# Two weight-gradient stores of a decode backward kernel, cut by rows into pieces

## The chip, the cores and the metric

The kernel runs on one core of a Trainium2 chip. The metric is the device time of one execution in microseconds; three runs of the kernel before took 736.78, 735.42 and 736.70 us, a median of 736.7. A profile of one further execution shows what each engine and each DMA queue did. The engines are TensorE (PE), VectorE (DVE), ScalarE (ACT), GpSimd (POOL) and SyncE (SP). The core has 16 DMA engines, and a DMA is issued from a queue of SyncE, GpSimd or ScalarE.

## The reference

One decode step (one token) through a parallel block, and its whole backward pass. In short:

```python
xn = layernorm(x)                                  # x: [1, 1, 640]
q = (xn @ wq) -> 32 heads of 128                   # wq: [640, 4096]
p = softmax(q . k_cache * 128**-0.5)               # k_cache, v_cache: [32 heads, 8192, 128]
o = p @ v_cache
out = x + o @ wo + (silu(xn @ w1) * (xn @ w3)) @ w2   # wo: [4096, 640], w1, w3: [640, 1728]
grads = vjp(out)(grad_out)   # of x, k_cache, v_cache, wq, wo, w1, w3, w2
```

Everything is bf16 in HBM. The caches are 64 MiB each, and their gradients are as large, so about 268 of the 303.5 MB that move are caches and cache gradients. The gradients of `wq` and `wo` are outer products: `d_wo` is the attention output times `grad_out`, `d_wq` is `xn` times the gradient of `q`.

## The kernel before

The work goes head by head, 32 heads in 8 groups of 4. A head's K and V (2 MB each, one DMA of 128 rows of 16 KB) lie in two of ten SBUF slots. `head(h)` transposes them on TensorE, makes scores, softmax and the sums for the gradients, and runs beside it, on VectorE, the outer products of the head before (`outers_a`, `outers_b`): these write the gradient of V and K over the slot itself. `store` (line 473) sends the slot to HBM from GpSimd's queue, and then asks SyncE's queue to load the next K or V into the same slot. That load waits until the store has landed. A separate block at head 2 does the gated MLP.

The order on each queue is the order of the program text (a manual schedule). GpSimd issues all stores of 128 rows and also the loads of the weights of later groups; SyncE issues the K and V loads. Each queue is served in order.

Per group there is a tile `wq_g` (128 rows, 5 pieces of 512 columns, 5,120 bytes a row) and a tile `wo_g` (128 rows, 4 pieces of 640 columns, also 5,120 bytes a row), each 640 KB, in three buffers that are used in turn. Their life:

- `load_group(g + 2)` (lines 109 to 114, called at line 698 in the last head of group g) loads both from GpSimd's queue. The buffer was group g-1's, so the load of `wq_g` waits until the `wq` gradient of group g-1 has landed, and everything behind it on GpSimd waits with it.
- `fin_wo(g)` (line 501, called from `side_v` in the first head of group g+1) writes the `wo` gradient over `wo_g` with four VectorE instructions and stores it by one DMA (line 505).
- `fin_wq(g, ci)` (line 507) does the same for `wq` in five steps, `ci` 0 to 4, spread over the second and third head of group g+1. The last is called from `side_m`, behind the store of V and ahead of the store of K of the head before, and issues one DMA (line 514).
- Group 7 is finished behind the last head, at lines 819 to 823.

Of the kernel before, what the change touches and what calls it, by code (L numbers as in the profile page):

```python
# [16 lines left out]
P = 128  # L17
# [4 lines left out]
def kernel(  # L22
# [22 lines left out]
    nc = tc.nc  # L45
# [8 lines left out]
    GH = 4  # L54
    NG = H // GH
    GW = GH * DH
# [23 lines left out]
    dwq_v = out_4.rearrange("(ci p) n -> p ci n", p=P)  # L80
    dwo_v = out_5.rearrange("(h p) c -> p h c", p=P)
# [110 lines left out]
    def out_row(vec, mat):  # L192
        k = mat.shape[0]
        for e in range(2):
            nc.tensor.matmul(acc[64 * e:64 * (e + 1), 0:DHALF], lhsT=vec.to_broadcast([k, 64]),
                             rhs=mat[:, e * DHALF:(e + 1) * DHALF], start=False, stop=True, skip_group_check=True)
# [292 lines left out]
    def fin_pe(g):  # L489
# [8 lines left out]
        for hh in range(GH):  # L498
            out_row(G_["od_bf"][:, hh, 0:1], G_["wo"][:, hh, :])

    def fin_wo(g):
        G_ = grp[g]
        for hh in range(GH):
            nc.vector.tensor_scalar(G_["wo"][:, hh, :], g_bc[:], G_["od"][:, hh, 0:1], None, ALU.mult)
        nc.gpsimd.dma_start(dwo_v[:, g * GH:(g + 1) * GH, :], G_["wo"][:])

    def fin_wq(g, ci):
        G_ = grp[g]
        wq_g, dqb = G_["wq"], G_["dqb"]
        nc.vector.scalar_tensor_tensor(wq_g[:, ci, :], wq_g[:, ci, :], 1.0, dqb, ALU.mult, ALU.mult,  # L510
                                       accum_out=dxa[:, ci, g:g + 1])
        nc.vector.tensor_scalar(wq_g[:, ci, :], dqb, xn_col[:, ci:ci + 1], None, ALU.mult)
        if ci == NC - 1:
            nc.gpsimd.dma_start(dwq_v[:, :, g * GW:(g + 1) * GW], wq_g[:])
            grp.pop(g)

    def wrow(wi, ci):
# [147 lines left out]
    def side_k(h):  # L665
        g, hh = divmod(h, GH)
        if hh == 1 and g > 0:
            fin_wq(g - 1, 0)
        elif hh == 2 and g > 0:
            fin_wq(g - 1, 3)  # L670
        elif hh == 3 and g + 1 < NG:
            prep_do(g + 1, 1)

    def side_m(h):
        g, hh = divmod(h, GH)
        if hh == 0 and g > 0:
            fin_od(g - 1)
        elif hh == 1 and g > 0:
            fin_wq(g - 1, 1)
        elif hh == 2 and g > 0:  # L680
            fin_wq(g - 1, 4)
        elif hh == 3 and g + 1 < NG:
            prep_do(g + 1, 2)
            prep_do(g + 1, 3)

    def side_v(h):
        g, hh = divmod(h, GH)
        if hh == 0 and g > 0:
            fin_wo(g - 1)
        elif hh == 1 and g > 0:  # L690
            fin_wq(g - 1, 2)
        elif hh == 2 and g + 1 < NG:
            prep_new(g + 1)
            prep_do(g + 1, 0)
        elif hh == 3 and g + 1 < NG:
            prep_cm(g + 1, hd[h]["m"][:, 324:324 + 4 * GH])
        if hh == 3 and g > 0 and g + 2 < NG:
            load_group(g + 2, nc.gpsimd)
# [120 lines left out]
    fin_od(NG - 1)  # L819
    fin_pe(NG - 1)  # L820
    fin_wo(NG - 1)
    for ci in range(NC):
        fin_wq(NG - 1, ci)
# [58 lines left out]
```

## Time and profile before

| what | us |
|---|---|
| median of three runs | 736.7 |
| the profiled execution | 735.86 |
| its span (first to last instruction) | 734.1 |
| PE busy / DVE busy / ACT busy / POOL busy | 601.6 / 460.3 / 375.5 / 64.7 |
| mean clock granted to TensorE | 0.917 of full |
| GpSimd's store of `wo_g`, issue to landing, median of 8 | 51.0 |
| GpSimd's store of `wq_g`, issue to landing, median of 8 | 48.6 |
| GpSimd's store of a K or V gradient, median of 64 | 45.2 |
| SyncE's load of K / of V, median of 32 each | 18.7 / 22.3 |

The page's second part cuts the span in 40 slices and gives the mean busy share of the 16 DMA engines in each, and the GB/s that they moved:

```profile
DMA  8999999999999999999999999999999999999991
GB/s 351 402 413 419 426 425 419 430 429 430 427 429 421 427 426 427 423 427 425 428 429 413 427 427 423 422 428 428 428 427 413 427 426 429 428 420 430 423 410 79
HBM read 151.34 MB, written 151.34 MB: 412 GB/s over the span
```

A DMA row of 9 in a slice means that the engines were busy 90% of the time or more. TensorE, the busiest compute engine, is busy 82% of the span.

### The profile page before, as it was taken

To read this page: it belongs to the slowest core of one execution; us is meant where nothing else is said; L and a number is where in the kernel's file an instruction comes from. 1 tells how busy PE (TensorE), PEld (TensorE's weight loads), DVE (VectorE), ACT (ScalarE), POOL (GpSimd) and SP (SyncE) were. 2 spreads that over 40 slices of the span, in tenths; PEclk is the share of its full clock that TensorE was granted. 3 is DMA by queue.
4 is the path that set the end of the run, shared out by engine and by line. 5 is a ranking of instruction groups with operands and counts; after the bars stand their busy time and mean duration, and the time that the engine had idled before them with its cause. 6 is when DMAs were issued, how large, how long until landed. Compare 5 with 4: busy or idle time off the path is not lost.

```text
span 734.1 us, 13013 instructions
## 1 busy us (share of the span) xinstructions
PE 601.6 (82%) x5186; PEld 374.7 (51%) x5193; DVE 460.3 (63%) x811; ACT 375.5 (51%) x727; POOL 64.7 (9%) x109
## 2 busy tenths in 40 slices
PE   4988589999899899988897869878798797886920
PEld 2556466665565566544554545544464454554510
DVE  4279637687867776767475555667367674664780
ACT  3641646655666666654454446544465453554500
POOL 0110100001011100200010100201002000001010
PEclk9996799999999999999899989999899998998955
DMA  8999999999999999999999999999999999999991
GB/s 351 402 413 419 426 425 419 430 429 430 427 429 421 427 426 427 423 427 425 428 429 413 427 427 423 422 428 428 428 427 413 427 426 429 428 420 430 423 410 79
DMA packets 27134, 303.52 MB, mean 413 GB/s; under 512 B 2798, under 2 KB 4146, under 8 KB 10434
## 3 DMA queue, kind: packets, MB, share of 16 engines
q0 software_dynamic: 14944, 160.52, 52.0%
q1 hardware_dynamic: 12126, 142.17, 46.0%
q8 instruction: 41, 0.67, 0.3%
q14 instruction: 19, 0.16, 0.1%
q10 hardware_dynamic: 4, 0.00, 0.0%
HBM read 151.34 MB, written 151.34 MB: 412 GB/s over the span
## 4 chain that ended last, share of the span: by engine, by line
DMA 30%; PE 28%; issue 17%; another core or an unknown queue 11%; DVE 7%; ACT 3%; POOL 1%; SPq 0%; POOLq 0%; ACTq 0%; DVEq 0%
DMA wo_g<-in_A_wo_dram 16%; PE pT L314 13%; DMA out_dram<-kv 8%; DMA kv<-in_A_k_cache_dram 4%; PE sA L335 4%; PE X L429 2%; PE dA L335 2%; DMA kv<-in_A_v_cache_dram 2%; DVE kv L462 2%; PE m L352 1%; ACT kv L624 1%; DVE side L253 1%; PE gu_ps L543 1%; PE dh_ps L554 1%
## 5 line engine op out<-in xcount | busy, mean ns | idle before, releaser
L316 ACT COPY KT<-pT 128x512 f32<-128x512 f32 x512 | 288.0, 588 | 231.0 <-PE pT L314 211.8
L314 PE MATMUL pT<-ident_f,kv 128*128 128x128 f32 x2048 | 304.6, 287 | 52.1 <-DMA kv<-in_A_k_cache_dram 34.5
L314 PEld LDWEIGHTS pT<-ident_f,kv 128*128 128x128 f32 x2048 | 234.2, 147 | 144.0 <-PE pT L314 52.1
L462 DVE TENSOR_TENSOR kv<-qd,U 128x4096 bf16<-128x4096 bf16 x64 | 146.0, 2283 | 0.0
L462 DVE TENSOR_TENSOR kv<-qd,P 128x4096 bf16<-128x4096 bf16 x64 | 143.6, 2284 | 0.0
L429 PE MATMUL X<-kv,Z 128*32 128x512 bf16 x1024 | 97.4, 414 | 1.4 <-DVE Z L446 1.4
L335 PE MATMUL dA<-KT,qz 128*32 128x512 bf16 x512 | 83.7, 406 | 0.0
L335 PE MATMUL sA<-KT,qz 128*32 128x512 bf16 x512 | 82.4, 401 | 0.0
L477 POOL DMA_DIRECT2D out_dram<-kv x64 | 34.7, 543 | 393.6 <-DVE kv L462 184.7
L412 DVE SCALAR_TENSOR_TENSOR U<-m,P 128x64 bf16<-128x64 f32 x32 | 7.4, 232 | 86.0 <-PE m L352 86.0
L429 PEld LDWEIGHTS <-Z 128*32 128x32 bf16 x1024 | 33.2, 101 | 35.1 <-issue 8.9
L335 PEld LDWEIGHTS <-qz 128*32 128x32 bf16 x1024 | 29.5, 95 | 40.4 <-issue 37.8
L378 DVE TENSOR_REDUCE mrow<-m 128x1 f32<-128x64 f32 x32 | 7.2, 224 | 56.1 <-PE m L352 56.0
L352 PE MATMUL m<-selc,KT 64*128 64x64 f32 x256 | 30.8, 244 | 11.7 <-ACT KT L342 11.7
L352 PEld LDWEIGHTS m<-selc,KT 64*128 64x128 f32 x256 | 21.8, 146 | 34.0 <-ACT KT L342 24.5
L253 DVE SCALAR_TENSOR_TENSOR side<-wo_g,g_bc 128x640 bf16<-128x640 bf16 x32 | 26.2, 820 | 16.6 <-DMA wo_g<-in_A_wo_dram 16.2
L372 ACT CAST qd<-pT 128x256 bf16<-128x256 f32 x32 | 11.9, 373 | 39.5 <-DVE kv L462 30.8
L385 DVE TENSOR_REDUCE negM<-m 128x1 f32<-128x128 f32 x32 | 9.3, 291 | 32.9 <-PE m L382 32.9
L510 DVE SCALAR_TENSOR_TENSOR wq_g<-wq_g,side 128x512 bf16<-128x512 bf16 x40 | 27.3, 682 | 0.0
L444 DVE SCALAR_TENSOR_TENSOR U<-m,P 128x128 bf16<-128x128 f32 x32 | 11.4, 356 | 15.4 <-PE m L442 15.4
L402 DVE RECIPROCAL rZ<-m 128x1 f32<-128x1 f32 x32 | 5.3, 166 | 24.2 <-PE m L396 24.2
L342 ACT COPY KT<-dA 64x512 f32<-64x512 f32 x32 | 18.6, 583 | 3.4 <-PE dA L335 3.4
(162 smaller groups left out, 392.1 us busy)
## 6 DMA issues: line engine op xcount, KB each, us to landing
out_dram<-kv POOLq DMA_DIRECT2D x64, 2048.0 KB, 45.2
kv<-in_A_k_cache_dram SPq DMA_DIRECT2D x32, 2048.0 KB, 18.7
kv<-in_A_v_cache_dram SPq DMA_DIRECT2D x32, 2048.0 KB, 22.3
out_dram<-wo_g POOLq DMA_DIRECT2D x8, 640.0 KB, 51.0
out_dram<-wq_g POOLq DMA_DIRECT2D x8, 640.0 KB, 48.6
wq_g<-in_A_wq_dram POOLq DMA_DIRECT2D x7, 640.0 KB, 30.8
wo_g<-in_A_wo_dram POOLq DMA_DIRECT2D x7, 640.0 KB, 34.9
kv<-in_B_w_dram SPq DMA_DIRECT2D x2, 1728.0 KB
```

The lines of the kernel that those rows point to most:

```text
L253: nc.vector.scalar_tensor_tensor(junk[:], G_["wo"][:, hh, :], 1.0, g_bc[:], ALU.mult, ALU.mult, accum_out=G_["do"][:, hh:hh + 1])
L314: nc.tensor.transpose(pT[:, k * P:(k + 1) * P], W3[:, 4 * c + k, :], ident_f[:])
L316: nc.scalar.copy(KT[:].rearrange("p k w -> p (k w)"), pT[:])
L335: nc.tensor.matmul(S_[kind][q:q + QW, :], lhsT=S_["qz"][:, o:o + QW], rhs=KTb[c][:, par, :], start=(c0 == 0 and par == 0), stop=(c0 == NCH ...
L342: nc.scalar.copy(XS[0:QH].rearrange("p k w -> p (k w)"), S_.pop(kind)[0:QH, :])
L352: nc.tensor.matmul(S_["m"][:, b0:b0 + 4 * J].rearrange("p (x c k t) -> p k x c t", x=4, k=4, t=2)[:, k], lhsT=XS[0:QH, k, :], rhs=selc[0:Q ...
L372: nc.scalar.copy(qd[:].rearrange("p a d -> p (a d)"), hd[h].pop("ps_r"))
L429: nc.tensor.matmul(xg["X"][q:q + QW, :], lhsT=Z[:, o:o + QW], rhs=W[:, N4 * i:N4 * (i + 1)], start=(slot == 0 and i < 4), stop=(slot == NS ...
L444: nc.vector.scalar_tensor_tensor(S_["U2"][:], S_["V"][:, 0:J].unsqueeze(2).to_broadcast([P, J, 2]), S_["m"][:, OC + NS:OC + NS + 1], S_["P ...
L462: nc.vector.tensor_tensor(dst[:, lo * DH:hi * DH].rearrange("p (j a b) -> p j a b", a=DH // 2, b=2), vec.rearrange("p (a b) -> p a b", b=2 ...
L477: nc.gpsimd.dma_start((dkc if kind == "K" else dvc)[h], t[:])
L510: nc.vector.scalar_tensor_tensor(wq_g[:, ci, :], wq_g[:, ci, :], 1.0, dqb, ALU.mult, ALU.mult, accum_out=dxa[:, ci, g:g + 1])
```

## The change

In groups 1 to 6 each of the two stores is cut by rows. The `wo` gradient goes out from GpSimd in three DMAs of 76, 2 and 50 rows. The `wq` gradient goes out in DMAs of 5 and 121 rows from GpSimd and one of 2 rows from SyncE (a negative number in the list). Groups 0 and 7 keep one DMA of 128 rows for each. The bytes, the tiles and what is computed stay as they are.

```diff
+    def store_group(g, dst, t, pieces):
+        lo = 0
+        for n in pieces:
+            eng = nc.gpsimd if n > 0 else nc.sync
+            eng.dma_start(dst[lo:lo + abs(n)], t[lo:lo + abs(n)])
+            lo += abs(n)
+        assert lo == P
+
+    DWO_PIECES = {g: (76, 2, 50) for g in range(1, NG - 1)}
+    DWQ_PIECES = {g: (5, 121, -2) for g in range(1, NG - 1)}
+
     def fin_wo(g):
...
-        nc.gpsimd.dma_start(dwo_v[:, g * GH:(g + 1) * GH, :], G_["wo"][:])
+        store_group(g, dwo_v[:, g * GH:(g + 1) * GH, :], G_["wo"], DWO_PIECES.get(g, (P,)))
 
     def fin_wq(g, ci):
...
         if ci == NC - 1:
-            nc.gpsimd.dma_start(dwq_v[:, :, g * GW:(g + 1) * GW], wq_g[:])
+            store_group(g, dwq_v[:, :, g * GW:(g + 1) * GW], wq_g, DWQ_PIECES.get(g, (P,)))
             grp.pop(g)
```

## The prediction

> **What bounds the kernel now.** I read the page's part on the slices first (shown above): from 20 to 700 us the 16 DMA engines never rest. So I asked how they finish, in windows of the end (columns: window, its length, busy time and instructions of PE, PEld, DVE, ACT, POOL, granted clock, DMA share, GB/s).
>
> ```profile
> 700.00:710.00 10.00, 1.81 (x12) 0.88 (x12) 8.78 (x18) 0.59 (x1) 1.83 (x3) 0.50 0.98 410
> 710.00:716.00 6.00, 0.93 (x3) 0.58 (x3) 4.20 (x18) 0.00 (x0) 0.87 (x1) 0.50 0.96 398
> 716.00:718.00 2.00, 0.00 (x0) 0.00 (x0) 0.00 (x0) 0.00 (x0) 0.00 (x0) 0.50 0.67 273
> 718.00:720.00 2.00, 0.00 (x0) 0.00 (x0) 0.00 (x0) 0.00 (x0) 0.00 (x0) 0.50 0.46 188
> 720.00:722.00 2.00, 0.00 (x0) 0.00 (x0) 0.00 (x0) 0.00 (x0) 0.00 (x0) 0.50 0.20 81
> 722.00:724.00 2.00, 0.00 (x0) 0.00 (x0) 0.00 (x0) 0.00 (x0) 0.00 (x0) 0.50 0.12 50
> 724.00:726.00 2.00, 0.00 (x0) 0.00 (x0) 0.00 (x0) 0.00 (x0) 0.00 (x0) 0.50 0.06 25
> 726.00:728.00 2.00, 0.00 (x0) 0.00 (x0) 0.00 (x0) 0.00 (x0) 0.00 (x0) 0.50 0.06 24
> 728.00:730.00 2.00, 0.00 (x0) 0.00 (x0) 0.00 (x0) 0.00 (x0) 0.00 (x0) 0.50 0.07 27
> ```
>
> All compute is over at 716. A share of 0.06 is one engine of 16, and 25 GB/s is one engine's rate (427/16 = 26.7). From about 724 to 730.7 **one single DMA engine** works off its part of the last stores while 15 are done. The DMA view of 724.3 to 730.7 says the same: 6.2% of 16 engines, all of it GpSimd's queue.
>
> ```profile
> DMA packets 26, 0.16 MB, mean 26 GB/s; under 512 B 3, under 2 KB 3, under 8 KB 21
> q0 software_dynamic: 26, 0.16, 6.2%
> ```
>
> The trace also keeps each packet's start, length and queue, though not its engine. An engine begins a packet 3 to 4 ns before its last one ends, so from 79 us on I chained the packets into sixteen lines (my own working; no view prints it). Ends: 716.1 to 717.1 for five lines, 717.7 to 722.0 for nine, 724.2 for one, 730.7 for the late one; mean 719.5. The late line has the same bytes as the rest; its 16 KB packets of GpSimd's queue took 641 ns on average (612 to 620 elsewhere), 335 of its 16 KB packets over 630 ns (19 to 43 elsewhere). No line rests before 700. So the time is **the late engine's total work**: 730.7, plus 3.4 to the span's end.
>
> What it does on the way: GpSimd waits for the `wq` store at each reload of the buffer, until the late engine has written its share.
>
> ```profile
> POOL wq_g L111 <- DMA out_dram<-wq_g: 126.5, 5, 33.8
> SPq L105 <- DMA out_dram<-kv: 605.0, 58, 22.2
> ```
>
> **The change part by part.** Bytes are equal. What moves is which engine carries which rows. A row of either gradient is 5,120 bytes, so 0.19 us of one engine (5,120 / 26.7 GB/s; the chained packets say 0.20). Today each engine carries 8 + 8 = 16 rows of the two stores of a group.
>
> How many engines does a piece use? The page's queue part shows small cases:
>
> ```profile
> q10 hardware_dynamic: 4, 0.00, 0.0%
> ```
>
> These are ScalarE's two loads of one row: two data packets and two completions, so one engine each. SyncE's stores behind 713 us, three of one row and one of four, left 14 packets: seven of data, seven completions. 64 rows of `w2` took sixteen, 128 rows sixteen. In every case the rows are shared out evenly over as many engines, up to 16, as divide them. If that holds, 76 rows go to 4 engines (19 each), 2 to 2 (1 each), 50 to 10 (5 each); 5 to 5 (1 each), 121 to 11 (11 each). 4 + 2 + 10 and 5 + 11 are both 16, so if each piece goes on where the last one ended, each gradient makes one round. Counted from the first engine, rows per group: four engines 19 + 1 = 20; the fifth 1 + 1 = 2; the sixth 1 + 11 = 12; the other ten 5 + 11 = 16; SyncE's two rows add one to each of the first two. Over six groups: fifth -84 rows, -16 us; sixth -24 rows, -4.6 us; first four +24, +4.6 us (with SyncE's rows the first two +30, +5.8 us); ten unchanged. No row shows such a piece from GpSimd, so the bounds for the late engine are -16 us (the fifth) and +5.8 us (one of the first two).
>
> Which is the late engine? It is none of the four that took SyncE's last stores of one and four rows: these landed by 719.7, while it was still at a K store. It is none of the eight that fetch TensorE's instructions (the 41 packets of queue 8 go round eight lines). Four lines are left. Three other lines carry the fetches of queue 14; two of these are in the first four, and the late line and one more of the last four hold the remaining ones. If those fetches sit on neighbours, the late line is the fifth or the sixth. I take that as the nearest reading, and that the pieces start at the first engine.
>
> [...]
>
> New end: the late engine at 714.7 (fifth) or 726.1 (sixth). The others: the second latest stays at 724.2; the first four, today at 716.3, 717.1, 717.9 and 719.8, come to 720.9 to 725.6. So the last one ends between 724.2 and 726.1; I take 725.0, **5.7 us earlier**.
>
> Costs. GpSimd issues three more DMAs a group, at 0.77 us for a whole one: 2.3 us, of a queue that is busy 64.7 of 734 us and stands waiting at L111 anyway: 0; without that cover 6 x 2.3 = 14 us at worst. Completion packets (at most 48 more a group, 9 ns each over 16 engines) are 0.2 us in all. SyncE's two rows are a new term. Its queue runs behind, since each load waits for the store of its slot. Its timeline (start, length, instruction):
>
> ```profile
> 460.30 0.33 SPq L105 DMA_DIRECT2D kv<-in_A_k_cache_dram  x1
> 476.16 0.33 SPq L105 DMA_DIRECT2D kv<-in_A_v_cache_dram  x1
> ```
>
> and GpSimd's, with the store and the reload that waits for it (start, length, instruction, and the rest ahead of it):
>
> ```profile
> 414.17 0.87 POOL L514 DMA_DIRECT2D out_dram<-wq_g  x1 [7.36 <-DMA wq_g<-in_A_wq_dram]
> ...
> 468.18 0.87 POOL L111 DMA_DIRECT2D wq_g<-in_A_wq_dram  x1 [33.77 <-DMA out_dram<-wq_g]
> ```
>
> The two rows stand behind the load of 460.30, so they issue at 460.6 and land behind its packets, on the first engines at 473 to 475 by the chained completions. L111 needs them, so it would move from 468.2 to about 474, with two K or V stores, the loads of the group and the `wo` store behind it; four times (groups 1 to 4 have a successor in their buffer). On the earliest engine the load's first packet began 8.8, 4.8, 4.2 and 2.9 us behind the issue at L111 in the four groups, so of some 5.5 us each 0, 0.7, 1.3 and 2.6 are uncovered there, 4.6 us at most. With a relieved late engine the K or V store ahead lands earlier (the slowest of the others reached these `wq` stores 4 to 11 us ahead of it), and the chain with it: I take 0, and keep +5 for the range.
>
> Sum: span 734.1 - 5.7 = 728.4. The profiled execution took 1.8 more than its span, 735.9, and the median of the runs is 0.8 above that: 728.4 + 1.8 + 0.8 = **731.0**.
>
> **The rivals.**
> 1. *Untouched* (0.19): the late engine is one of the ten with 16 rows. It ends at 730.7 as before, whatever the others do; even 5 us of rest on the early ones fits in their 6 to 14 us of margin. 736.7, within 1. For it: four candidates are left and the neighbour argument is weak.
> 2. *Loaded* (0.17), the slower side: the pieces do not start at the first engine, and the late one is among the four with 20 rows. It then has 24 more rows, +4.6 us, or +5.8: 741.3 to 742.5. It decides from two rows a group on (2.3 us; 0.2% is 1.5 us). For it: no row shows where a piece begins. Against: from the first engine on it cannot be.
> [...]
>
> **Chances.** Forecast 0.56, its own range 729.5 to 732.5. About 0.2% (1.5 us) is what a measurement of this kernel tells from no change. Faster: 0.56 plus 0.04 of the even spread, 0.60. Within 0.2%: 0.19. Slower: 0.17 + 0.04 = 0.21. The range takes the forecast's and the untouched case, with part of the stall: 729.0 to 739.0; the loaded case is left out.
>
> **What would show it.** The stretch with a share of 0.06 at the end is gone or below 2 us; the wait at L111 falls well below 126.5 us in groups 4 to 7; DMA share stays at 0.98 or more until 700. Queue 1 gains 72 packets (six times ten of 1,024 bytes and two completions). A stretch at 0.06 as long as before means untouched; longer by some 5 us, loaded; a DMA share below 0.97 around the waits at L111 means that SyncE's two rows starve the queue.

## The result and the profile after

The changed kernel takes **769.3 us** (median of 4 runs, 766.2 to 770.9) against 736.2 before (median of 4 beside them, 735.4 to 736.8): ratio 1.0445, 95% interval 1.0407 to 1.0484. It is 33 us slower. The forecast was 731.0, and the slower rival went to 742.5 only.

From the page after: the slices' rate and the queues.

```profile
span 769.1 us, 13051 instructions
...
GB/s 352 399 415 416 429 423 427 427 428 428 427 426 420 403 412 420 412 388 392 399 335 407 399 397 407 355 398 399 391 406 350 416 392 383 424 418 417 340 409 100
DMA packets 29703, 303.57 MB, mean 395 GB/s; under 512 B 5282, under 2 KB 6720, under 8 KB 13002
...
q0 software_dynamic: 17440, 160.49, 52.7%
q1 hardware_dynamic: 12198, 142.23, 44.2%
```

The rate stays near 427 GB/s (416 to 429) from 58 us until about 230 us, the time of the first pieces, and then falls into dips of 335 to 355. The windows say how (columns as in the prediction):

```profile
205.00:245.00 40.00, 38.34 (x341) 23.61 (x338) 30.45 (x46) 23.84 (x48) 6.57 (x10) 0.96 1.01 424
245.00:310.00 65.00, 61.90 (x556) 38.49 (x555) 47.27 (x81) 41.39 (x85) 7.44 (x11) 1.00 1.01 412
330.00:400.00 70.00, 48.42 (x401) 30.04 (x403) 34.77 (x56) 30.41 (x60) 4.22 (x7) 0.85 0.97 385
400.00:420.00 20.00, 17.33 (x156) 10.82 (x152) 14.26 (x26) 11.46 (x23) 5.49 (x8) 1.00 0.96 370
...
500.00:590.00 90.00, 69.59 (x563) 42.45 (x565) 49.00 (x79) 41.55 (x83) 9.57 (x15) 0.91 0.98 390
590.00:680.00 90.00, 73.07 (x606) 44.94 (x606) 52.84 (x87) 44.56 (x90) 10.30 (x16) 0.89 1.01 404
...
755.00:760.00 5.00, 0.00 (x0) 0.00 (x0) 0.00 (x0) 0.00 (x0) 0.00 (x0) 0.50 0.15 64
760.00:765.00 5.00, 0.00 (x0) 0.00 (x0) 0.00 (x0) 0.00 (x0) 0.00 (x0) 0.50 0.12 50
```

The kernel before has, over a like stretch:

```profile
330.00:420.00 90.00, 75.69 (x614) 45.13 (x619) 54.57 (x95) 45.46 (x91) 8.15 (x13) 0.91 1.01 425
500.00:590.00 90.00, 75.14 (x628) 45.73 (x627) 53.26 (x88) 46.58 (x93) 7.59 (x12) 0.92 1.01 425
590.00:680.00 90.00, 73.40 (x612) 45.62 (x614) 53.44 (x90) 44.75 (x89) 6.47 (x11) 0.92 1.01 427
```

The reading to learn is the last two columns together. From 590 to 680 the share is 1.01 in both kernels, so the engines are busy all the time, yet they move 404 in place of 427 GB/s: the packets themselves take longer. From 330 to 400 the share falls too (0.97): there engines also rest. From the packet records (my own working, as no view adds it up): 364 of the 8,192 packets of 16 KB in GpSimd's queue took over 0.9 us, against 52 before and a usual 0.61; packet time above the usual for its size, in that queue, is 26.5 us an engine (4.9 before); rest until 30 us from the end is 10.1 us an engine (none before). The two grew by 21.6 and 10.1 us, together 31.7 of the 33.

GpSimd's waits (total us, times, longest):

```profile
POOL wq_g L111 <- DMA out_dram<-wq_g: 151.3, 5, 40.1
...
POOL out_dram L477 <- issue: 74.1, 11, 18.2
POOL out_dram L505 <- DMA out_dram<-kv: 59.6, 12, 9.3
POOL out_dram L477 <- DMA out_dram<-wo_g: 45.5, 5, 12.9
```

The wait at L111 grew from 126.5 to 151.3, where the prediction wanted it "well below". The last two lines are waits of one DMA for an older one ("issue" is idle time for which the profile shows no releaser). The semaphore records show what for: GpSimd's DMAs go round eight semaphores (111 to 118), so a DMA waits until the one eight before it has landed. The longest of these waits, 18.2 us, ends with the store issued at 363.26 us; the `wo` piece issued at 309.17 us, eight DMAs before, landed at 362.69 (own working). This text calls that a place in flight. And SyncE's two rows stand behind a load, as foreseen (start, length, instruction); L111 issues at 399.67:

```profile
386.11 0.33 SPq L105 DMA_DIRECT2D kv<-in_A_k_cache_dram  x1
386.54 0.83 SPq L505 DMA_DIRECT2D out_dram<-wq_g  x1
400.92 0.33 SPq L105 DMA_DIRECT2D kv<-in_A_v_cache_dram  x1
```

### The profile page after: what moved, and what is told of

It reads as the page before. It is cut to its first block, busy times and chain, and to the rows that moved or that the text cites. A ratio compares the mean times of both kernels' runs of the same rounds, so it can differ in the third digit from the quotient of the medians.

```text
span 769.1 us, 13051 instructions
## 1 busy us (share of the span) xinstructions
PE 605.8 (79%) x5186; PEld 377.0 (49%) x5193; DVE 460.5 (60%) x811; ACT 375.0 (49%) x727; POOL 80.8 (11%) x127
## 3 DMA queue, kind: packets, MB, share of 16 engines
q0 software_dynamic: 17440, 160.49, 52.7%
q1 hardware_dynamic: 12198, 142.23, 44.2%
## 4 chain that ended last, share of the span: by engine, by line
DMA 48%; PE 33%; DVE 6%; issue 4%; ACT 3%; another core or an unknown queue 1%; POOL 0%; SPq 0%; ACTq 0%; POOLq 0%; DVEq 0%
DMA out_dram<-kv 25%; PE pT L314 15%; DMA wo_g<-in_A_wo_dram 10%; DMA out_dram<-wq_g 6%; DMA out_dram<-wo_g 5%; PE sA L335 4%; PE dA L335 3%; PE X L429 3%; DVE kv L462 2%; DMA kv<-in_A_k_cache_dram 2%; PE m L352 2%; ACT KT L316 1%; ACT kv L635 1%; PE gu_ps L554 1%
## 5 line engine op out<-in xcount | busy, mean ns | idle before, releaser
L314 PE MATMUL pT<-ident_f,kv 128*128 128x128 f32 x2048 | 307.9, 289 | 66.3 <-DMA kv<-in_A_k_cache_dram 59.8
L314 PEld LDWEIGHTS pT<-ident_f,kv 128*128 128x128 f32 x2048 | 236.9, 149 | 156.9 <-issue 67.3
L429 PE MATMUL X<-kv,Z 128*32 128x512 bf16 x1024 | 102.3, 430 | 1.4 <-DVE Z L446 1.4
L429 PEld LDWEIGHTS <-Z 128*32 128x32 bf16 x1024 | 34.4, 104 | 38.1 <-issue 13.8
L253 DVE SCALAR_TENSOR_TENSOR side<-wo_g,g_bc 128x640 bf16<-128x640 bf16 x32 | 26.2, 820 | 18.5 <-DMA wo_g<-in_A_wo_dram 18.2
L111 POOL DMA_DIRECT2D wq_g<-in_A_wq_dram x7 | 6.2, 891 | 151.6 <-DMA out_dram<-wq_g 151.3
L342 ACT COPY KT<-dA 64x512 f32<-64x512 f32 x32 | 18.7, 584 | 4.6 <-PE dA L335 4.6
```

What stands on the lines that cost most here:

```text
L253: nc.vector.scalar_tensor_tensor(junk[:], G_["wo"][:, hh, :], 1.0, g_bc[:], ALU.mult, ALU.mult, accum_out=G_["do"][:, hh:hh + 1])
L314: nc.tensor.transpose(pT[:, k * P:(k + 1) * P], W3[:, 4 * c + k, :], ident_f[:])
L342: nc.scalar.copy(XS[0:QH].rearrange("p k w -> p (k w)"), S_.pop(kind)[0:QH, :])
L429: nc.tensor.matmul(xg["X"][q:q + QW, :], lhsT=Z[:, o:o + QW], rhs=W[:, N4 * i:N4 * (i + 1)], start=(slot == 0 and i < 4), stop=(slot == NS ...
```

## The experiments

Four theories. **A**: unequal shares throw the engines out of step, and that alone costs. **B**: each further DMA takes one of eight places in flight. **C**: SyncE's rows land late and hold GpSimd at L111. **D**, a guess formed on the way from e10's packets of up to 2.64 us: a piece of few rows makes several engines read the same part of the on-chip buffer, and they slow each other there. e1 to e9, e11 and e12 were each timed once, which is good to some 2 us (the kernel before ran from 734.3 to 738.5 in all).

**First four: one part of the change at a time.** Only these lines are edited:

```diff
e1_even   wo (64, 16, 48)   wq (16, 96, -16)     # minus: by SyncE
e2_wo     wo (76, 2, 50)    wq whole
e3_wq     wo whole          wq (5, 121, -2)
e4_sync   wo whole          wq (112, -16)
```

> Groups 1 to 6 with as many DMAs as the changed kernel (three and two from GpSimd, one from SyncE), but row counts that divide by 16 (64, 16 and 48 rows; 16 and 96 with 16 by SyncE), so that every engine keeps equal shares. Theory A (unequal shares throw the engines out of step, and their GpSimd packets then slow each other): about 736, within 5. Theory B (GpSimd has at most eight DMAs in flight, and three more small ones a group hold the big stores back): 755 to 770. Theory C (SyncE's rows land late and hold GpSimd at the reload of the buffer): 745 to 755, as in the run with SyncE's piece alone.

> Only the wo gradient is cut (76, 2, 50); wq leaves whole. Theory A: most of the loss stays, 750 to 765, since four engines carry 19 rows. Theory B: two of the three extra DMAs a group, about two thirds of the loss, 755 to 760. Theory C: no loss, 730 to 737.

> Only the wq gradient is cut (5, 121, and 2 by SyncE). Theory A: shares of 1 against 11 rows, a smaller step, 740 to 755. Theory B: one extra DMA a group, about a third of the loss, 745 to 750. Theory C: the whole loss, 765 to 770.

> wq leaves as 112 rows by GpSimd and 16 by SyncE, wo whole: equal shares, no extra DMA on GpSimd, only the rows by SyncE. Theories A and B: 734 to 738. Theory C: 750 or more.

Measured, beside 737.4 of the kernel before: 756.1, 751.3, 739.9, 750.9. No single theory holds: e1 has only even shares and costs 18.7 us (against A), e2 has nothing on SyncE and costs 13.9 (against C alone), e4 has no further GpSimd DMA and costs 13.6 (against B alone).

**Next four: SyncE taken out.**

```diff
e5_wo_even  wo (64, 16, 48)  wq whole
e6_wq_even  wo whole         wq (16, 112)
e7_act      wo (76, 2, 50)   wq (5, 121, -2)     # minus: by ScalarE
e8_wq_act   wo whole         wq (5, 121, -2)     # minus: by ScalarE
...
-            eng = nc.gpsimd if n > 0 else nc.sync
+            eng = nc.gpsimd if n > 0 else nc.scalar   # e7, e8
```

> The wo gradient alone leaves in three GpSimd DMAs, of 64, 16 and 48 rows, which divide evenly over 16 engines; the wq gradient in one, as before. Nothing on SyncE. A (unequal shares throw the engines out of step and cost time): no unequal share is left, so 736 to 738, the time before. B (each further GpSimd DMA takes one of the eight places in flight, so the queue is held): as the same count of DMAs with 76, 2 and 50 rows, 750 to 758, since the relief of 8 rows a group on the late engine is missing here too or more. C (SyncE's rows come late and hold L111): no such rows, 736 to 738.

> The wq gradient alone leaves in two GpSimd DMAs of 16 and 112 rows, evenly shared; nothing on SyncE. One further GpSimd DMA a group instead of two. A and C: 736 to 738. B: one place in flight in place of two, so about half of what two cost, 741 to 747.

> The changed kernel with its pieces as they are, but the last 2 rows of the wq gradient leave by ScalarE's queue in place of SyncE's, behind no load. C: the longest wait at L111 falls from 40 us to about 28 (what it is with the wq gradient in one piece), and the time by the 13 us that SyncE's rows cost alone, or more: 748 to 757. B: only the two further wo DMAs and one for wq are left, 750 to 758. If neither holds and the unequal shares do it all (A): 766 to 771, unchanged.

> The wq gradient alone leaves as 5 and 121 rows by GpSimd and 2 rows by ScalarE's queue; the wo gradient in one piece. With 5, 121 rows and SyncE's 2 rows this was 739.9. C: the hold at L111 goes, the relief of 7 rows a group on the late engine stays, so 728 to 733, below the kernel before. B: one further GpSimd DMA costs 5 or more, so 735 to 740. A: 740 as it was, or more.

Measured, beside 737.1: 741.2, 740.6, 760.9, 742.4. As many DMAs cost 4.1 us with 64, 16, 48 rows and 13.9 with 76, 2, 50, so their number is not it (against B). In the whole change, SyncE's rows are 8.5 us (769.3 to 760.9), so C is a part; but with the wq gradient alone there is nothing to win (e3 739.9; e8 742.4, where C wanted 728 to 733), although the wait at L111 falls from 158.8 to 127.9 us between them. Some 24 us stay without SyncE.

**Next four: where does the imbalance cost?** e9 turns the pieces of wo round in every second group; e10 is the kernel before with one split store near its end; e11 is e7 with the wo store moved right ahead of the wq store; e12 has four further, even DMAs.

```diff
e9_mirror     wo (76, 2, 50) in groups 1, 3, 5 and (50, 2, 76) in 2, 4, 6;  wq whole
e12_more      wo (32, 16, 16, 16, 48)   wq whole
e10_kv, in store():
-        nc.gpsimd.dma_start((dkc if kind == "K" else dvc)[h], t[:])
+        dst = (dkc if kind == "K" else dvc)[h]
+        lo = 0
+        for n in ((5, 121, 2) if (kind, h) == ("K", H - 2) else (P,)):
+            nc.gpsimd.dma_start(dst[lo:lo + n], t[lo:lo + n])
+            lo += n
e11_together, from e7_act (the same line is taken out of fin_wo), in fin_wq():
         if ci == NC - 1:
+            store_group(g, dwo_v[:, g * GH:(g + 1) * GH, :], G_["wo"], DWO_PIECES.get(g, (P,)))
             store_group(g, dwq_v[:, :, g * GW:(g + 1) * GW], wq_g, DWQ_PIECES.get(g, (P,)))
```

> The wo gradient alone in three GpSimd DMAs: 76, 2 and 50 rows in groups 1, 3 and 5, and 50, 2 and 76 in groups 2, 4 and 6; the wq gradient in one piece. The engines that get 19 rows in one group get 5 in the next, so over the six groups the most loaded engines have 24 more rows of 0.2 us than even ones in place of 66: 8.4 us less than with 76, 2, 50 in all groups (751.3). If only each engine's total counts: 741 to 743. If each group's own imbalance is lost in that group (A, 11 rows of 0.2 us, six times, not made good later): 749 to 753.

> The kernel before, with one change: the K store of head 30, behind which no reload waits, leaves as 5, 121 and 2 rows in place of 128. The late engine, the fifth, gets 1 of its 8 packets of 16 KB, so 7 x 0.64 = 4.5 us less; eleven others get 3 more (1.8 us). If the end is one late engine's total work and the loss of the changed kernel came from its six groups: 0.993 to 0.996 of before, 731.5 to 734. If three pieces out of step cost as in a group (2 us or more each): 735 to 738.

> The pieces of the changed kernel with the last 2 wq rows on ScalarE (760.9), but the wo gradient's three pieces are issued right ahead of the wq gradient's, so that the two uneven shares follow each other at once instead of 40 us later. A (engines out of step between the two): 742 to 750. B (five GpSimd DMAs in a row take five of eight places in flight): 760 or more.

> The wo gradient alone in five GpSimd DMAs of 32, 16, 16, 16 and 48 rows, all shared evenly; four further DMAs a group where 64, 16, 48 has two (741.2). A: no more than about 1 us a DMA, 741 to 746. B (each takes a place in flight): twice the two's cost or more, since more than half of the places are taken, 745 to 755.

Measured, beside 737.0: 746.0, 744.1, 749.2, 739.5; e10, of four executions, has a ratio of 1.009 (1.0061 to 1.0119). Four further even DMAs a group cost 2.5 us, not more than two did: **B is out** as the cause of the groups' loss. e9 lies between the two figures given. e11 gains 11.6 us on e7 and its wait at L111 falls from 124.3 to 58.9 us; it doesn't tell whether the shorter imbalance, the later issue or fewer meetings of engines did that. The surprise is e10, one store split by the prediction's own rule, where nothing is reloaded: 7 us slower in place of 4.5 faster. Its windows:

```profile
690.00:700.00 10.00, 7.87 (x77) 4.53 (x74) 7.21 (x11) 3.95 (x9) 1.54 (x3) 1.00 0.97 399
700.00:710.00 10.00, 1.81 (x12) 0.88 (x12) 8.81 (x15) 0.59 (x1) 1.88 (x3) 0.54 1.00 304
```

From 700 to 710 the share is 1.00 and the rate 304 GB/s (410 before, shown in the prediction). In the packet records from 700 to 715 us the packets of 16 KB take up to 2.64 us, over four times the usual 0.61. That is where theory D comes from.

**Next four: shares and rows told apart.** e13 and e14 are e10 with other pieces, each an equal share; e16 splits by heads, so that each DMA has all 128 rows; e15 splits only behind the last reload.

```diff
e13_half   K store of head 30 as (64, 64);   e14_eight   as (16,) * 8
e15_last   wo (76, 2, 50) and wq (5, 121, 2) in group 7 alone
e16_cols, from the kernel before:
-        nc.gpsimd.dma_start(dwo_v[:, g * GH:(g + 1) * GH, :], G_["wo"][:])
+        for lo, hi in ((0, 2), (2, 3), (3, GH)) if 0 < g < NG - 1 else ((0, GH),):
+            nc.gpsimd.dma_start(dwo_v[:, g * GH + lo:g * GH + hi, :], G_["wo"][:, lo:hi, :])
```

> The kernel before, with the K store of head 30 as two DMAs of 64 rows: every engine has 4 + 4 rows, 8 as before. A (only unequal shares cost): 736 to 738, packets of 16 KB at 0.61 us as before. D (engines that read the same part of the buffer share its rate, as the packets of up to 2.64 us behind the split 5, 121, 2 suggest): if 64 rows reach half of the parts, two engines share each, the store's eight packets take 1.22 us in place of 0.61 on every engine, and the time rises by up to 8 x 0.61 = 4.9 us: 739 to 743. [...]

> The same store as eight DMAs of 16 rows: one row an engine each, 8 in all as before. A: 736 to 738. A cost for each DMA, some 1 us as the four even ones suggest: up to 743. D: if 16 rows reach a quarter of the parts, four engines share one, packets take up to 4 x 0.61 = 2.44 us, and the time rises by more than with halves, up to 8 x 1.83 = 14.7 us where all engines stay in step: 742 to 752.

> The pieces of the changed kernel only in the last group, behind which no transfer of its queue follows: wo as 76, 2, 50 and wq as 5, 121, 2 rows, all by GpSimd; groups 1 to 6 whole. The fifth engine, late by 6.5 us at the end of the kernel before, gets 2 of 16 rows: 14 x 0.2 = 2.8 us less. If the prediction's rule holds wherever nothing behind it can be held up: ratio 0.995 to 0.998. A and D: rows on shared parts are slow here too, but engines that are early by 6 us or more can take that: 0.995 to 1.003.

> The wo gradient of groups 1 to 6 in three GpSimd DMAs, split by heads (2, 1 and 1) and not by rows, so that each has all 128 rows, 8 an engine. Two further DMAs a group, as with 64, 16 and 48 rows (741.2). A and D: no cost but the DMAs themselves, 736 to 738. A cost of each DMA in flight (B): 740 to 742, as with 64, 16, 48.

Measured, beside 736.5, as ratios with their intervals: e13 1.0087 (1.0072 to 1.0102), e14 1.0064 (1.0045 to 1.0082), e15 1.0013 (1.0005 to 1.0022), e16 1.0003 (0.9993 to 1.0012). The halves give every engine its eight rows as before (64 rows of `w2` took sixteen engines in the kernel before) and cost 6.4 us: **A can't say that, D can**. Their windows:

```profile
700.00:705.00 5.00, 0.20 (x2) 0.11 (x1) 5.00 (x3) 0.17 (x1) 0.57 (x1) 0.60 1.01 343
705.00:710.00 5.00, 1.81 (x12) 0.88 (x12) 3.85 (x11) 0.58 (x1) 1.30 (x2) 0.50 0.99 330
...
725.00:730.00 5.00, 0.00 (x0) 0.00 (x0) 0.00 (x0) 0.00 (x0) 0.00 (x0) 0.50 0.06 26
730.00:735.00 5.00, 0.00 (x0) 0.00 (x0) 0.00 (x0) 0.00 (x0) 0.00 (x0) 0.50 0.06 26
```

Busy engines at 330 to 343 GB/s while the halves leave, and then one engine alone from 725 to 738.1. e13's 6.4 us are more than D's bound of 4.9, which reckoned with the store's own eight packets. From 695 us on all packets of 16 KB together took 2.7 us an engine more than usual (0.2 before; own working). Chained back from the end, the engine that comes last lost 6.9 of them and the others 0.2 to 4.7; where packets are slow they no longer follow each other within 3 to 4 ns, so this split suggests, and does not show, why one engine is left so far behind.

The eighths show the slow packets as well (46 of 16 KB over 2.1 us, none before), and more of them: 7.5 us an engine from 695 us on. Yet they cost less time than the halves, where D said more: that expectation missed. But e14 differs from e13 in a second thing. Its windows, and two of GpSimd's issues:

```profile
710.00:715.00 5.00, 0.71 (x3) 0.58 (x3) 3.75 (x17) 0.00 (x0) 0.50 (x1) 0.50 0.48 82
715.00:720.00 5.00, 0.22 (x1) 0.00 (x0) 0.28 (x1) 0.00 (x0) 1.85 (x4) 0.50 0.56 69
```

```profile
711.77 0.50 POOL L480 DMA_DIRECT2D out_dram<-kv  x1 [4.78 <-DMA out_dram<-kv]
717.24 0.48 POOL L480 DMA_DIRECT2D out_dram<-kv  x1 [4.97 <-DMA out_dram<-kv]
```

From the fourth piece on each waits for a place in flight, so the eight are issued over 23 us (694.6 to 717.2), the last store of the kernel at 720.5 (712.6 before), and from 710 to 720 us about half of the engines rest. So e14's time can't be set beside e13's as a dose of D, and here a count of DMAs does hold GpSimd up.

e16 has as many GpSimd DMAs as e5 and e2 and costs nothing measurable, though GpSimd does wait for places in flight (last line):

```profile
POOL wq_g L111 <- DMA out_dram<-wq_g: 121.9, 5, 33.3
...
POOL out_dram L506 <- DMA out_dram<-kv: 34.4, 7, 6.7
```

**Last two: the on-chip buffer taken out.** What remains of A is asked with the same unequal pieces read from DRAM.

```diff
-        store_group(g, dwo_v[:, g * GH:(g + 1) * GH, :], G_["wo"], DWO_PIECES.get(g, (P,)))
+        store_group(g, dwo_v[:, g * GH:(g + 1) * GH, :],
+                    wo_v[:, g * GH:(g + 1) * GH, :] if 0 < g < NG - 1 else G_["wo"], DWO_PIECES.get(g, (P,)))
e17_d2d         wo whole         wq whole
e18_d2d_uneven  wo (76, 2, 50)   wq whole
```

> In groups 1 to 6 the store of the wo gradient is left out; a copy of the same size from the input wo in DRAM to the output takes its place, in one piece of 128 rows. The control for the next run: 733 to 742, as such a copy may take longer or shorter than the store.

> The same copy from DRAM to DRAM as 76, 2 and 50 rows, so the first four engines have 11 rows more than even in each group and the fifth 7 fewer, and none of the three pieces reads the on-chip buffer. From the buffer this cost 14 us (751.3 against 737.4). A (unequal shares cost by themselves): 10 to 15 more than the copy in one piece. D (only engines that meet in the buffer): what the first four's totals give, 66 rows of 0.2 us = 13.2 less the 11 to 14 us by which they end ahead of the late engine, so 0 to 3 more, or less by the late engine's relief.

Measured, beside 736.5: 734.9 and 737.8, ratios 0.9979 (0.9967 to 0.9991) and 1.0018 (1.0008 to 1.0028). Both runs leave the wo gradient of groups 1 to 6 out. The pieces that cost 13.9 us out of the buffer cost 2.9 us out of DRAM, inside the 0 to 3 that the totals give. A hold on GpSimd's queue isn't the difference: its wait at L111 is 104.8 us in e18 and 108.2 in e2, its wait for places in flight at L505 64.4 and 64.6. One window of e2, then the same of e18:

```profile
500.00:590.00 90.00, 72.82 (x608) 44.67 (x606) 52.80 (x87) 45.34 (x91) 9.39 (x14) 0.92 1.00 414
```

```profile
500.00:590.00 90.00, 75.59 (x643) 46.66 (x643) 55.85 (x91) 46.03 (x92) 9.98 (x15) 0.94 1.01 422
```

With the same shares and the same number of DMAs, the busy engines keep 422 GB/s when the pieces come from DRAM, and 414 when they come from the buffer (425 in the kernel before).

The table sets the runs side by side. "Packets" is by how much the time above the usual of GpSimd's packets grew, "rest" by how much the engines' rest grew until 30 us from the end, both in us an engine against the kernel before (own working; rest to within 1 us).

| run | against before, us | packets | rest |
|---|---|---|---|
| e17 copy whole | -1.6 | -0.7 | 0 |
| e18 copy 76, 2, 50 | +1.3 | 1.6 | 0 |
| e16 three DMAs of 128 rows | +0.7 | 0.9 | 0 |
| e12 wo in five even pieces | +2.5 | 2.4 | 1 |
| e3 wq 5, 121, 2 by SyncE | +2.6 | 5.4 | 0 |
| e6 wq 16, 112 | +3.5 | 6.5 | 0 |
| e5 wo 64, 16, 48 | +4.1 | 5.6 | 0 |
| e8 wq 5, 121, 2 by ScalarE | +5.3 | 7.3 | 1 |
| e9 wo turned round | +9.0 | 7.5 | 1 |
| e11 as e7, wo beside wq | +12.3 | 9.9 | 2 |
| e4 wq 112, 16 by SyncE | +13.6 | 7.8 | 4 |
| e2 wo 76, 2, 50 | +13.9 | 7.3 | 4 |
| e1 all even, 16 by SyncE | +18.7 | 15.1 | 3 |
| e7 change, ScalarE for SyncE | +23.8 | 17.0 | 6 |
| after | +33 | 21.6 | 10 |

Every split by rows out of the buffer in the table lengthens the packets, by 2.4 to 21.6 us an engine, with equal shares too (2.4 to 6.5 without SyncE). In the dearer runs the engines also rest. That is most of what sets e2 apart from e5, whose packets are slowed by 5.6 us in place of 7.3: unequal shares out of the buffer cost 9.8 us more than equal ones (each timed once), where out of DRAM they cost 2.9 in all. Why the two together make the engines rest isn't shown, so something of A is left.

## Why the prediction was wrong

**What bounds the kernel.** Right for the kernel before: its end is one late DMA engine, which works alone for the last 6 us.

**How rows are shared out.** Right. In the packets after, each wq gradient shows 11 packets of 3,072 bytes and 5 of 1,024: 121 rows on eleven engines and 5 on five. Queue 1 gained the 72 packets that were named (12,126 to 12,198).

**Which engine is late, and where the pieces start.** Right, and partly by luck: the prediction itself calls its neighbour argument weak. Chaining the packets after as far as 403 us (own working), the line with the slow GpSimd packets is the one that got two rows, and it had as many packets behind it as the others, while two of the first four lagged. e15 shows it without a long chain: its last engine is alone from 727 us on and gets, behind its last K or V packet, one row of each gradient, which are the two rows of the fifth. So the relief in rows came. But that last K or V packet ends at 730.4 us there, 727.4 before, with 11 packets of 16 KB over 0.9 us since 695 us in place of 1, and the 2.8 us of relief are gone.

**"Bytes are equal. What moves is which engine carries which rows."** This is the step that failed, with the price under it: 0.19 to 0.20 us a row, whichever engine carries it. The sum knew only how many rows an engine has. A row's price also depends on how its DMA is cut out of the buffer: with e13's equal halves 43 packets of 16 KB take about twice as long (over 1.1 us, none before) and the time rises by 6.4 us, while splits that keep all 128 rows (e16) or leave the buffer (e18) pay at most what the sum says. So the change's pieces cost, without SyncE, 13.9 us (wo) and 5.3 us (wq) alone and 23.8 us together (e7). The prediction worked only with 4.6 to 5.8 us of load on the first engines, which their early end was to absorb. That the source of the rows decides is shown (e16, e18); which rows slow each other isn't.

The runs show that few rows from the buffer were slow: 330 to 343 GB/s in place of 410 while the halves left, 43 packets of 16 KB over 1.1 us for 64 rows (e13), and 46 over 2.1 us, 3.4 times the usual, for 16 rows (e14). That engines meet in one part of the buffer is D's guess. That 64 rows reach half of the parts and 16 rows a quarter, on which D's figures for e13 and e14 rest, no run shows; these packets are what was measured in their place. They don't follow the count of rows simply: e12's five even pieces cost less than e5's three (2.5 and 4.1 us, each timed once).

**"Three more GpSimd DMAs a group = 0."** Right to within what e16 can tell (0.9993 to 1.0012 for two more). The eight places in flight are seen in the waits (34.4 us at L506 in e16), and in the groups they are not the loss. The 0.2 us for further small packets was too little: those of 4 to 16 bytes take 1.6 us an engine more (0.9 before, 2.5 after; own working), and 2,118 of the further ones have 12 or 16 bytes, sizes that don't occur before.

**SyncE's two rows, "I take 0, and keep +5".** L111 does come later, as worked out. In the whole change they cost 8.5 us (e7), in the wq gradient alone nothing that single executions can tell (e3, e8); 16 rows by SyncE instead of GpSimd cost 10 us (e4 against e6). So 0 was too low. The reason given for it, that a relieved engine lets the chain run ahead, failed with the slower packets: the wait grew to 151.3 us. How the price depends on the rest isn't settled.

**Rivals.** Each of them went by rows an engine. *Loaded* had the right sign for a reason that didn't occur, and stopped at 742.5. The named sign, "a DMA share below 0.97 around the waits at L111", did show in one stretch (0.96 at 370 GB/s from 400 to 420) but was put down to SyncE alone. The even spread that the chances name (0.04 faster, 0.04 slower) no run shows: after the change 121 rows went over eleven engines and 5 over five.

No version that stores all gradients was measurably faster than the kernel before. e15, which puts the pieces where nothing follows, has its last packet of GpSimd's queue at 732.3 (730.6 before) and is 0.13% slower.

## What to carry to other kernels

A DMA of fewer than 128 rows from the on-chip buffer wasn't a fraction of a whole one here: with equal shares, e13's halves made 43 packets of 16 KB take over 1.1 us in place of 0.61 and cost 6.4 us. Split along the row's length, so that each piece keeps all rows (+0.7 us in e16, not told from nothing), or measure first what a split by rows costs. Read the DMA share together with the rate: a share of 1.00 at 304 in place of 410 GB/s went with slower packets (e10, up to 2.64 us), a share of 0.97 at 385 GB/s with engines that also rest (after, from 330 to 400 us). To ask where a late engine's work may go, split one transfer at the end first; that single experiment (e10) shows here that the sign was wrong.

## What the runs showed of the hardware

One K store of 2 MB, sent as 64 and 64 rows with equal shares, made 43 packets of 16 KB take over 1.1 us in place of 0.61 and cost 6.4 us; as 5, 121 and 2 rows, packets took up to 2.64 us. GpSimd's queue has 2,496 packets more after the change (14,944 to 17,440), for fewer bytes (160.52 to 160.49 MB): 2,088 of 16 bytes and 30 of 12, where the kernel before has none, 354 more of 4 bytes and 24 more of data. The count is the one that comes out if each engine that a piece leaves idle gets one small packet for each packet of a busy one, and each further DMA sixteen of 4 bytes at its end (own working). A copy of the wo gradient's size from DRAM to DRAM in one piece was no slower than the store from the buffer (734.9 against 736.5), and in pieces of 76, 2 and 50 rows it took 737.8.
